# Leaving out zero products in front of four transposes in a fused attention and feed-forward kernel

## The chip, the cores and the metric

The kernel runs on one core of a Trainium2 chip. The metric is the device time of one execution in microseconds (us); unless another unit is given, every time below is in us. A core has five engines that run side by side, each with its own instruction queue worked off in order: TensorE (PE, matrix products; its weight loads are shown apart as PEld), VectorE (DVE), ScalarE (ACT), GpSimd (POOL) and SyncE (SP). Products land in PSUM, eight banks of 128 partitions; VectorE and ScalarE bring them from there to SBUF. Transfers are issued by an engine's queue and carried out by 16 DMA engines. TensorE's clock is granted by a throttle; the profile shows the granted share (1.00 is full speed).

## The reference

Attention with squared relu in place of softmax (8 batches, 12 heads, 448 positions, 64 wide), followed by a gated feed-forward layer over all 3584 tokens:

```python
scores = scale * np.matmul(q, k.transpose(0, 1, 3, 2))
attn = np.maximum(scores, 0.0) ** 2 / S
x = np.matmul(attn, v)              # heads side by side: 3584 x 768
gate = np.maximum(x @ w_gate, 0.0)
val = x @ w_val
out = (gate * val) @ w_out
```

Inputs and output are float32; the kernel computes in bfloat16 with float32 sums.

## The kernel before

The kernel goes batch by batch. A batch's heads are worked on in pairs (`hp` 0 to 5), and two pairs make a `qd` (0 to 2). q and k come in with tokens on the partitions (`qn`, `kn`) and are needed with the 64 features of a head on the partitions (`kqT`). For the first two batches TensorE makes that transposition; from the third batch on VectorE regroups the rows (`regroup`, L180, into `kr` and `qr`) and a transposing DMA on SyncE's queue does the rest.

Each batch has 21 score tiles (7 of each `qd`). A tile is four products of 64 by 64 that run together in the four quarters of TensorE's array (`mm4`), into two PSUM banks. `relu2` then takes it to SBUF: ScalarE's relu (L232) and VectorE's square (L233), which together make `attn`. `value_passes` multiplies `attn` with v, seven passes for a `qd`, and the result x is copied to SBUF (L640 by VectorE, L653 by ScalarE); `exchange` (L261) copies its halves to the other partitions. `gv_unit` makes the gate and value products from x, twelve passes for each of twelve units; L320 and L321 take them out. For later batches the attention of batch b is dealt out between the gate units of batch b-1, and the output products (`out_pair`) follow every second batch.

The change lies in `first_batch`, where no earlier batch's products fill TensorE. There the order is written out by hand, and `keep_in_program_order` holds every instruction to it. Three pairs of PSUM banks (0, 2, 4) take the tiles in turn, so that tile n can start when the relu of tile n-3 has read its banks; relu buffers `r_sb` are four, so that the relu of tile n waits for the square of tile n-4. Banks 6 and 7 take the transposes of pairs 2 to 5 in turn, and later the value products. The steps, in TensorE's order:

- twelve pairs of products of a tile of zeros (`blank`) while the first rows are loaded, then pairs 0 and 1's transposes (`first_transposes`), then four more pairs of zero products
- tiles 0 to 18, and after tiles 3, 5, 7 and 9 the transposes of pairs 2, 3, 4 and 5 (16 products with an identity, `transposes`, L208), which VectorE copies to `kqT` (L209); two pairs of zero products stand in front of each
- after tiles 12 and 17 the value products of the first and second `qd`
- tiles 19 and 20, the third `qd`'s value products and the first gate passes in between

Tile 7 is the first of `qd` 1 and needs the copies of pairs 2 and 3; tile 14 those of pairs 4 and 5. `idle_matmuls(ps, n)` issues n pairs of products, each half of the array's columns, of zeros with zeros into a bank that is overwritten afterwards; nobody reads them.

The loads are all issued by GpSimd (L116), in an order written ahead of the loops: q and k of the first batch, v, gate weights, then the second batch and more weights. They take eight semaphores in turn, so that a load is issued only when the load eight before it has landed. `load_qk(2)`, the third batch's q and k, stands right behind `first_batch` in that queue, behind the last gate weights; `regroup` of the third batch (L180) waits for it in VectorE's queue, between the second batch's squares and the gate's products.

Of the kernel before, what the change touches and what calls it, by code (L numbers as in the profile page):

```python
# [16 lines left out]
def kernel(  # L17
# [50 lines left out]
    def pin(ins):  # L68
        return tc.keep_in_program_order(ins)
# [4 lines left out]
    def mm2(o, l, r, start, stop):  # L74

        for c, p in HALVES:
            mm(o[p], l[:, p], r, start, stop)
# [124 lines left out]
    def transposes(b, hp, bank):  # L202

        ps = bank.bitcast(BF16).rearrange("p (t c) -> p t c", t=2)
        for t, nat in enumerate((kn_b[b % NB], qn_b[b % NB])):
            for i in range(4):
                for h2, half in HALVES:
                    pin(nc.tensor.transpose(ps[half, t, i * 128:i * 128 + 128], nat[:, 2 * hp + h2, i, :], ident))  # L208
        pin(nc.vector.tensor_copy(T_b[b % NB][:, :, hp, :], ps[:, :, 0:S]))  # L209

    def first_transposes(numbers):

        for n, (hp, t) in zip(numbers, ((0, 0), (0, 1), (1, 0), (1, 1))):
            ps = banks[:, n, :].bitcast(BF16)
            for i in range(4):
                for h2, half in HALVES:
                    pin(nc.tensor.transpose(ps[half, i * 128:i * 128 + 128],
                                            (kn_b, qn_b)[t][0][:, 2 * hp + h2, i, :], ident))
            o = T_b[0][:, t, hp, :]
            if (hp, t) == (1, 0):  # L220
                pin(nc.scalar.activation(o, ps[:, 0:S], AF.Copy))
            else:
                pin(nc.vector.tensor_copy(o, ps[:, 0:S]))
# [6 lines left out]
    def relu2(src, dst):  # L230
        r = rpool.tile([128, 2, S], BF16, name="r_sb")
        pin(nc.scalar.activation(r, src, AF.Relu))  # L232
        pin(nc.vector.tensor_tensor(dst, r, r, ALU.mult))  # L233
# [8 lines left out]
    def tile_of(b, n, ps):  # L242

        qd, i = divmod(n, NC)
        T = T_b[b % NB]
        a = i * 128 if i < 4 else (i - 4) * 128 + 64
        mm4([ps[:, r, :S] for r in range(2)], lambda r, c: T[:, 0, pair_of(b, 2 * qd + c), a:a + 64],
            lambda r, c: T[:, 1, pair_of(b, 2 * qd + c), :], True, True)
        return ps[:, :, :S], attn_of(b, qd)[:, 2 * i:2 * i + 2, :]

    def value_passes(b, qd, ps, i0, i1):

        attn, v_sb = attn_of(b, qd), v_b[b % NB]
        for i in range(i0, i1):
            mm4([ps[:, r, :S] for r in range(2)], lambda r, c: v_sb[:, 2 * qd + c, i, :],
                lambda r, c: attn[:, 2 * i + c, :], i == 0, i == NC - 1)

    def exchange(b, qd):
        x0, x1 = (x_of[b][e][qd] for e in range(2))
        for (_, p), (_, other) in zip(HALVES, HALVES[::-1]):  # L260
            pin(nc.vector.tensor_copy(x1[p], x0[other]))  # L261
# [19 lines left out]
    def idle_matmuls(ps, n):  # L281

        for _ in range(n):
            mm2(ps[:, :S], blank[:, 0:128], blank, True, True)
# [310 lines left out]
    def first_batch(units):  # L595


        def passes(u, n):
            for _ in range(n):
                units[u].pop(0)()  # L600

        def bank(n):
            return banks[:, n, :]

        def tile(n, at=None):
            todo.append(tile_of(0, n, sc_first() if at is None else banks[:, at:at + 2, :]))

        todo = []

        def scored():  # L610
            relu2(*todo.pop(0))

        def second_by_dve():
            src, dst = todo.pop(1)
            r = rpool.tile([128, 2, S], BF16, name="r_sb")
            pin(nc.vector.tensor_scalar(r, src, 0.0, None, ALU.max))
            scored()
            pin(nc.vector.tensor_tensor(dst, r, r, ALU.mult))

        idle_matmuls(bank(6), 12)  # L620
        first_transposes((6, 7, 5, 4))
        idle_matmuls(bank(2), 4)
        tile(0)
        tile(1)
        both = banks[:, 6:8, :]
        for n in range(2, 19):
            tile(n)
            if n in (3, 5, 7, 9):
                hp = n // 2 + 1
                idle_matmuls(bank(6 + hp % 2), 2)  # L630
                transposes(0, hp, bank(6 + hp % 2))
            if n in (12, 17):
                value_passes(0, n // 14, both, 0, NC)
            if n == 2:
                second_by_dve()
            elif n > 3:
                scored()
            if n in (12, 17):
                qd = n // 14
                pin(nc.vector.tensor_copy(x_of[0][0][qd], both[:, :, :S]))  # L640
        tile(19)
        scored()
        passes(0, 4)
        scored()
        tile(20, 0)
        scored()
        value_passes(0, 2, both, 0, 4)
        scored()
        passes(1, 4)
        value_passes(0, 2, both, 4, NC)  # L650
        exchange(0, 0)
        exchange(0, 1)
        pin(nc.scalar.activation(x_of[0][0][2], both[:, :, :S], AF.Copy))  # L653
        exchange(0, 2)
        for n in range(4):
            for u in range(2):
                passes(u, 2)
# [83 lines left out]
    new_x(0)  # L741
    units = gv_units(0)
    first_batch(units)
    load_qk(2)
    load_v(2)
# [90 lines left out]
```

## Time and profile before

| | us |
|---|---|
| median of 3 runs | 408.68 (407.84 to 408.9) |
| the profiled execution | 406.69 |
| its span, first to last instruction | 404.9 |
| TensorE busy in the span | 393.0 (97%) |
| VectorE busy | 303.9 (75%) |
| ScalarE busy | 244.3 (60%) |

A row of a timeline gives start, length, engine, line, operation, tiles written and read, and a count; a bracket gives the idle time before it and what ended that. Matmuls are pipelined, so lengths of neighbours overlap, and the distance between starts tells more of the rate than a length does. The chain of waits is the chain of work that ended last, followed back from the end: at each step to what released it. A table by stretches gives each engine's busy time and count of instructions, the granted clock and what the transfers moved.

### The profile page before, as it was taken

Reading aid. Unit: us, or ns where it says so; the run is one execution under the profiler, and the core shown is the slowest. Engines: PE = TensorE matmul, PEld = TensorE weight load, DVE = VectorE, ACT = ScalarE, POOL = GpSimd, SP = SyncE. Lnnn points to the kernel's source line nnn. Section 1 sums busy time; section 2 is a strip of 40 time slices with the busy share of each in tenths; the row PEclk is TensorE's granted clock in tenths of the full one; section 3 lists DMA queues with packets and bytes.
Section 4 is the critical chain, followed back from the end, with each engine's and each line's share of the span. In section 5 each row is a group of like instructions: output and inputs, shape, how many; then the busy total and the mean of one; then the engine's idle time right before and its main releaser. Section 6 shows DMA issues by size and latency. Waiting matters only on the chain.

```text
span 404.9 us, 16604 instructions
## 1 busy us (share of the span) xinstructions
PE 393.0 (97%) x7392; PEld 276.3 (68%) x7392; DVE 303.9 (75%) x532; ACT 244.3 (60%) x358; POOL 96.0 (24%) x164
## 2 busy tenths in 40 slices
PE   7899999999999999999999999999999999999994
PEld 3567767779776666666677677687777766777773
DVE  5985895599944786787833988988889869997651
ACT  3962984797334776877324889899873243434221
POOL 8833500610213601205244030020003120000240
PEclk9999999999999999999999999999999999999999
DMA  9999999799726993978946459561002350000154
GB/s 157 176 196 196 197 194 135 122 203 162 119 83 177 118 161 70 139 112 99 191 86 173 103 88 123 103 95 14 3 3 50 83 145 3 3 2 3 42 135 101
DMA packets 90984, 44.17 MB, mean 109 GB/s; under 512 B 55424, under 2 KB 89952, under 8 KB 90912
## 3 DMA queue, kind: packets, MB, share of 16 engines
q0 software_dynamic: 51136, 28.58, 49.5%
q1 hardware_dynamic: 39104, 13.99, 17.9%
q8 instruction: 58, 0.95, 0.9%
q10 hardware_dynamic: 672, 0.54, 0.5%
q14 instruction: 14, 0.11, 0.1%
HBM read 47.19 MB, written 11.01 MB: 144 GB/s over the span
## 4 chain that ended last, share of the span: by engine, by line
PE 79%; DVE 7%; DMA 5%; ACT 3%; issue 2%; SPq 2%; POOL 0%; DVEq 0%; ACTq 0%; POOLq 0%
PE ps L72 78%; DVE attn L233 4%; DMA kn<-in_k_dram 3%; ACT r_sb L232 3%; SPq L409 2%; DMA qn<-in_q_dram 1%; PE ps L208 1%; DMA out_dram<-attn 1%; DVE x L640 1%; DVE attn L399 0%; DVE kqT L209 0%; DVE hT L321 0%; ACT g_sb L320 0%; DVE kr L180 0%; DVE qr L180 0%
## 5 line engine op out<-in xcount | busy, mean ns | idle before, releaser
L72 PE MATMUL ps<-x,gv 64*64 64x448 bf16 x3552 | 203.5, 349 | 0.5 <-ACT r_sb L232 0.3
L72 PEld LDWEIGHTS <-gv 64*64 64x64 bf16 x4032 | 139.0, 107 | 54.8 <-issue 2.8
L232 ACT ACTIVATE r_sb<-ps 128x896 bf16<-128x896 f32 x167 | 147.9, 926 | 18.6 <-PE ps L72 15.1
L233 DVE TENSOR_TENSOR attn<-r_sb 128x896 bf16<-128x896 bf16 x167 | 102.2, 623 | 31.3 <-ACT r_sb L232 24.5
L72 PE MATMUL ps<-kqT 64*64 64x448 bf16 x672 | 67.9, 351 | 3.8 <-ACT r_sb L232 2.8
L72 PEld LDWEIGHTS <-hT 128*64 128x64 bf16 x1056 | 56.2, 110 | 20.8 <-issue 1.7
L409 POOL DMA_DIRECT2D out_dram<-attn x60 | 31.6, 531 | 154.0 <-DVE attn L399 121.2
L395 ACT ACTIVATE attn<-ps 128x384 f32<-128x384 f32 x64 | 28.9, 451 | 63.9 <-PE ps L72 63.3
L72 PE MATMUL ps<-wo,hT 128*64 128x384 bf16 (+1 forms) x720 | 53.9, 306 | 0.0
L321 DVE TENSOR_TENSOR hT<-ps,g_sb 128x448 bf16<-128x448 f32 x72 | 44.5, 619 | 9.2 <-ACT g_sb L320 8.6
L320 ACT ACTIVATE g_sb<-ps 128x448 bf16<-128x448 f32 x72 | 39.2, 546 | 18.5 <-PE ps L72 18.1
L399 DVE TENSOR_TENSOR attn<-ps,attn 128x384 f32<-128x384 f32 (+1 forms) x48 | 22.7, 503 | 33.4 <-ACT attn L395 19.4
L72 PEld LDWEIGHTS <-vn 64*64 64x64 bf16 (+1 forms) x840 | 30.9, 107 | 12.8 <-issue 2.3
L72 PEld LDWEIGHTS <-kqT 64*64 64x64 bf16 x672 | 27.0, 106 | 18.4 <-issue 8.4
L72 PE MATMUL ps<-attn,vn 64*64 64x448 bf16 x672 | 36.9, 350 | 0.1
L513 ACT ACTIVATE kqT<-ps 128x896 f32<-128x896 f32 x18 | 16.5, 918 | 25.0 <-PE ps L72 25.0
L116 POOL DMA_DIRECT2D vn<-in_v_dram x36 | 23.8, 681 | 23.0 <-DMA wo<-in_moe_w_out_dram 9.6
L677 POOL COPY flag<-kqT 128x1 bf16<-128x1 bf16 x12 | 3.1, 261 | 103.0 <-DMA kqT<-kr 75.9
L72 PE MATMUL ps<-o_ring,hT 128*64 128x384 bf16 (+1 forms) x336 | 25.8, 306 | 0.1
L517 DVE TENSOR_TENSOR kqT<-ps,kqT 128x896 f32<-128x896 f32 x18 | 19.5, 1084 | 5.9 <-PE ps L72 4.2
L266 ACT ACTIVATE x<-ps 128x448 bf16<-128x448 f32 x15 | 8.2, 544 | 14.4 <-PE ps L72 14.4
L261 DVE COPY x<-x 64x896 bf16<-64x896 bf16 x36 | 14.7, 408 | 2.0
(104 smaller groups left out, 289.4 us busy)
## 6 DMA issues: line engine op xcount, KB each, us to landing
out_dram<-attn SPq DMA_DIRECT2D x48, 96.0 KB, 2.6
out_dram<-attn POOLq DMA_DIRECT2D x46, 96.0 KB, 2.4
kn<-in_k_dram POOLq DMA_DIRECT2D x7, 384.0 KB, 5.9
qn<-in_q_dram POOLq DMA_DIRECT2D x7, 384.0 KB, 7.8
vn<-in_v_dram POOLq DMA_DIRECT2D x14, 192.0 KB, 9.1
gv<-in_moe_w_gate_dram POOLq DMA_DIRECT2D x6, 384.0 KB, 11.3
gv<-in_moe_w_val_dram POOLq DMA_DIRECT2D x6, 384.0 KB, 10.9
wo<-in_moe_w_out_dram POOLq DMA_DIRECT2D x2, 1152.0 KB, 12.3
```

The lines of the kernel that those rows point to most:

```text
L72: pin(nc.tensor.matmul(o, lhsT=l, rhs=r, start=start, stop=stop, skip_group_check=True))
L116: pin(nc.gpsimd.dma_start(out=o, in_=i))
L232: pin(nc.scalar.activation(r, src, AF.Relu))
L233: pin(nc.vector.tensor_tensor(dst, r, r, ALU.mult))
L261: pin(nc.vector.tensor_copy(x1[p], x0[other]))
L320: pin(nc.scalar.activation(g_sb, o[0], AF.Relu, scale=float(out_scale)))
L321: pin(nc.vector.tensor_tensor(hT[:, mf, col:col + S], o[1], g_sb, ALU.mult))
L395: pin(nc.scalar.activation(out_of(t, r, c), bank(P, t), AF.Copy))
L399: pin(nc.vector.tensor_tensor(o, bank(Q, t), o, ALU.add))
L409: pin(engines[c].dma_start(out=rows[:, c0:c1, :], in_=src))
L513: pin(nc.scalar.activation(held(n, j), both(PQ[n][0]), AF.Copy))
L517: pin(nc.vector.tensor_tensor(k, both(PQ[n][1]), k, ALU.add))
```

## The change

```diff
@@ -627,7 +627,6 @@
             tile(n)
             if n in (3, 5, 7, 9):
                 hp = n // 2 + 1
-                idle_matmuls(bank(6 + hp % 2), 2)
                 transposes(0, hp, bank(6 + hp % 2))
             if n in (12, 17):
                 value_passes(0, n // 14, both, 0, NC)
```

Each of the four calls issued two pairs of products of zeros, 64 columns by 448, with a weight load each: 16 products and 16 weight loads in all. The zero products at the start and ahead of tile 0 stay. No other engine has an instruction more, fewer or in another place.

## The prediction

> **What bounds the kernel now.** I read the granted clock first (1.00 throughout), then the chain of waits over the whole span:
>
> ```profile
> 12.41 0.64 DVE kqT L209
> 13.09 0.88 PE ps L72 x7
> 14.46 0.62 DVE kqT L209
> 15.08 1.07 DVE attn L233 x2
> ...
> 27.13 5.98 PE ps L72 x118
> ...
> 42.18 12.79 DMA kn<-in_k_dram
> ...
> 58.31 152.84 PE ps L72 x2926
> ```
>
> The columns are start, length, and what held the chain. Up to 14.46 the chain goes to and fro between TensorE and VectorE. From there VectorE alone sets it, squares and copies end to end, until 27.13. Then TensorE sets it, then a load of k rows for the third batch that lands at 42.18 + 12.79 = 54.97, and from 58.31 TensorE again. So the removed work lies in a stage that is bound by VectorE, and behind that stage stands a transfer.
>
> Next, TensorE's and VectorE's timelines of the first batch:
>
> ```profile
> 9.59 0.38 PE L72 MATMUL ps<-kqT 64*64 64x448 bf16 x4 [0.64 <-ACT r_sb L232]
> 9.90 0.57 PE L72 MATMUL ps<-blank 128*64 128x448 bf16 x4
> 10.30 0.39 PE L208 MATMUL ps<-ident,kn 128*64 128x128 bf16 x8
> 10.53 0.39 PE L208 MATMUL ps<-ident,qn 128*64 128x128 bf16 x8
> ```
> ```profile
> 12.41 0.62 DVE L209 COPY kqT<-ps 128x896 bf16<-128x896 bf16 x1 [0.29 <-PE ps L208]
> 12.95 1.15 DVE L233 TENSOR_TENSOR attn<-r_sb 128x896 bf16<-128x896 bf16 x2
> 14.46 0.62 DVE L209 COPY kqT<-ps 128x896 bf16<-128x896 bf16 x1 [0.36 <-PE ps L208]
> ```
>
> The lengths hold a pipeline's tail, so what a group costs TensorE is the distance between starts: 10.30 - 9.90 = 0.40 for the four zero products. The brackets say that VectorE stood idle for 0.29 and 0.36 until transposes were done. The view shows no other wait for transposes in this stage.
>
> **The change, part by part.** It removes 4 groups of 4 zero products with their weight loads, 32 TensorE instructions, and adds and moves nothing; the order on every engine is otherwise as it was. On TensorE that is 4 x 0.40 = 1.6 (9.90 to 10.30, 11.35 to 11.75, 13.40 to 13.80, 14.85 to 15.25). I followed it through the stage, start by start:
> - Pair 2's transposes may start at 9.90. Their q rows are heads 4 to 7, whose second load lands at 10.11 (issued 4.95, landing 5.16 later, in the trace's records). The eight k transposes run first, 0.23, so q's start at 10.13 and lose nothing. VectorE's copy of pair 2 goes from 10.96 to 10.89 only, as the operation before it takes until then.
> - Pair 3's transposes gain two groups, 0.80: done near 11.57 in place of 12.37. The copy follows at 11.96, behind a square, in place of 12.41: 0.45.
> - Tile 7 (13.09) waits for that copy and gains 0.45, pair 4's transposes 0.45 + 0.40 = 0.85: copy at 13.60 in place of 14.46. From here VectorE would be 0.85 ahead.
> - ScalarE must keep up. Its relus start 0.80 apart when nothing holds them. Single starts show three delays: 10.23 to 11.28 and 13.69 to 14.78 (for TensorE's tiles, 0.25 and 0.29 over) and 14.78 to 15.70 (for VectorE's square that frees a buffer, 0.13 over). They vanish, which makes 0.67; after them relus go on at 0.80 as before, and no tile comes late, since a tile follows the relu that frees its bank. The last square follows the last relu within 0.1, so the stage gains the smaller: 0.67, plus the 0.06 of slack between the two, about **0.7**. The work at 27.13 starts near 26.4.
>
> So 0.9 of the 1.6 is lost at once, to VectorE's and ScalarE's own pace. The other 0.7 meets this:
>
> ```profile
> core 0: us, PE busy (x) PEld busy (x) DVE busy (x) ACT busy (x) POOL busy (x), PEclk, DMA share, GB/s
> 16.00:28.00 12.00, 10.05 (x178) 6.12 (x171) 11.85 (x23) 10.45 (x13) 5.98 (x9) 1.00 1.46 194
> 28.00:42.00 14.00, 13.96 (x318) 10.07 (x317) 7.59 (x14) 4.23 (x8) 5.51 (x8) 1.00 1.48 196
> 42.00:55.00 13.00, 12.79 (x268) 9.21 (x263) 11.06 (x20) 12.34 (x17) 5.20 (x8) 1.00 1.48 198
> ```
> ```profile
> 54.51 0.62 DVE L233 TENSOR_TENSOR attn<-r_sb 128x896 bf16<-128x896 bf16 x1 [0.19 <-ACT r_sb L232]
> 55.10 0.56 DVE L180 COPY kr<-kn 128x1536 bf16<-128x1536 bf16 x1
> 55.57 0.62 DVE L233 TENSOR_TENSOR attn<-r_sb 128x896 bf16<-128x896 bf16 x1
> ```
>
> From 28 to 55 TensorE is full (26.75 of 27), so its work moves 0.7 earlier. At 55.10 VectorE's regrouping copy (L180) waits in its queue for the k rows of 54.97, and behind it in the same queue come a square, a product, another regrouping and a copy of x (57.65), for which TensorE waits at 58.31. The rows do not land sooner: the transfers move 194 to 198 GB/s in each stretch from 16 to 55, one load behind another, and the k load waits 12 us in that line between issue and landing. Now the copy starts 0.12 after the landing, of which about 0.05 is VectorE's own queue (its operations start 0.53 to 0.54 apart, here 0.59 after the square). So of the 0.7 no more than some **0.05** passes 55; VectorE stands idle for the rest. Nothing behind 55 changes.
>
> Sum: the profiled execution has a span of 404.9 and 1.8 around it, 406.69 in all; it becomes 406.64. It lies 2.0 under the median of the three runs shown, so I carry the difference over: 408.68 - 0.05 = 408.6. The bounds of the gain are 0 and 0.7 (if the landing did move along).
>
> **The clock.** The zero products are work for the clock gate, so their absence may cost more than they do. What the trace shows of the gate:
>
> ```profile
> 398.00:401.30 3.30, 1.44 (x24) 1.12 (x20) 0.85 (x2) 0.34 (x2) 0.00 (x0) 1.00 0.58 137
> 401.30:404.70 3.40, 0.00 (x0) 0.00 (x0) 0.00 (x0) 0.00 (x0) 0.00 (x0) 1.00 0.51 132
> 404.76:404.90 0.14, 0.00 (x0) 0.00 (x0) 0.00 (x0) 0.00 (x0) 0.00 (x0) 0.50 0.00 0
> ```
>
> A stretch with 1.44 busy of 3.30 (44%) did not cost the clock; it fell to 0.50 at 404.7, over 5 us after the last product. After the change the stretch from 9.5 to 15.2 holds 8 tiles x 0.19 and 8 x 0.225 of transposes, 3.3 of 5.7 or 58%, with no pause as long as 1. On that count it stays up, and I cost the clock at 0. But without the transposes only 1.5 of 5.7 is left, 27%, under anything that the trace shows to be enough.
> [...] No stretch of this trace has transposes without other products to tell.
>
> **The rivals.**
> 1. The gain survives 55. For it: the chain names a VectorE square as what released the issue at 41.45, so an earlier square might mean an earlier load. Against it: the 12 us in line, and the full rate. Time: 408.68 - 0.7 = 408.0.
> 2. The zero products did not run in TensorE's own time, and leaving them out moves nothing. Against it: 0.40 between starts, four times. It would give 408.7, as the forecast, so it has no chance of its own.
> 3. Slower: the clock falls somewhere between 12 and 19. Place: tiles, transposes and two blocks of value products run at half speed. Price: the zero products at the start of the span, before the clock rises, start 0.37 a pair (1.16, 1.54 and so on to 5.27) in place of 0.19, and it took some 4 us of unbroken work, from 1.16 to 5.3, for the clock to rise. Four such us from 15.2 hold six tiles and the first block of value products (7 x 0.19 = 1.3), which grows to 2.6 and holds up ScalarE, which has 0.35 to spare there (tile 13 is done at 18.57, its relu starts at 18.92): about +0.9. If the clock stays low until 27, the 7.6 of products from 15.8 (11 tiles, 21 value passes and 8 gate passes, 40 x 0.19) need 15.2 in 11.3: +3.9; and 4 more us at half speed behind 27 cost another 2. Less 0.7: +0.2 to +5.2. I take +2.0, nearer the short fall: 410.7. It is not absorbed at 55, since TensorE is full before it and VectorE has but 0.05 there. It decides once it costs more than 0.7. Only the thin 27% speaks for it; the 58% and the row of 44% speak against it.
>
> **How the numbers follow.** Forecast (no change, 408.6; own range 407.9 to 409.3) 0.48; the gain survives 0.10; the clock falls 0.42: the price of being wrong on how transposes count is one-sided, and the trace leaves that count open. A measurement here tells about 0.3% (1.2 us) from no change. Faster by more: 0.03 from the first rival's upper part and 0.02 from scatter: 0.05. Slower by more: 0.34 from the clock, 0.01 from scatter: 0.35. Within: 0.60. The range goes from 407.7 (rival 1 with some scatter) to 411.0, just over the clock's 410.7, and leaves out its long tail.
>
> **What would show it.** Right: no blank rows after 9.5; the L209 copies without TensorE idle before them, near 11.96 and 13.60; TensorE's start at 27.13 near 26.4; L180 still at 55.1 with about 0.6 of VectorE idle before it, released by the k load; 58.3 unmoved. Wrong on the landing: L180 earlier than 54.8. Wrong on the clock: a granted clock below 1.00 between 9 and 30, tiles starting 0.38 apart, and TensorE at 27.13 or later.

## The result and the profile after

The changed kernel takes 406.53 (median of 18 runs, 405.58 to 408.55), the kernel before, run beside it, 408.33 (18 runs, 406.87 to 409.97). The ratio is 0.9963 with a 95% interval of 0.9948 to 0.9977: faster by 0.37%, some 1.5 us (the two medians themselves lie 1.80 apart), where no change that can be measured was forecast. The profiled execution after has 406.18 and a span of 404.4, only 0.5 less than the profiled one of before; that one lies 0.2 under all 18 timed runs of its kernel, so the two spans alone understate the gain.

The chain of waits of the changed kernel (start, length, what held the chain):

```profile
11.81 0.55 DVE kqT L209
12.36 1.07 DVE attn L233 x2
13.42 0.60 DVE kqT L209
...
26.46 5.95 PE ps L72 x118
...
41.82 12.85 DMA kn<-in_k_dram
...
54.79 0.10 DVE kr L180
...
58.01 6.74 PE ps L72 x134
64.75 0.80 issue
65.55 169.10 PE ps L72 x3204
```

VectorE holds the chain through the transposes now: between the copies (L209) the chain no longer passes through TensorE. The load of k rows is still there, it lands at 41.82 + 12.85 = 54.67 (54.97 before), and TensorE goes on at 58.01 (58.31 before). The two lines at the end are new: TensorE stops for 0.80 at 64.75 and nothing that the profile shows releases it.

The timelines of the changed kernel show TensorE's two groups of transposes of pair 2, then VectorE's copies of pairs 3 and 4 and its regrouping (the bracket is the idle time before, and what ended it):

```profile
9.59 0.41 PE L208 MATMUL ps<-ident,kn 128*64 128x128 bf16 x8
10.20 0.41 PE L208 MATMUL ps<-ident,qn 128*64 128x128 bf16 x8 [0.20 <-DMA qn<-in_q_dram]
```
```profile
11.73 0.62 DVE L209 COPY kqT<-ps 128x896 bf16<-128x896 bf16 x1
13.40 0.62 DVE L209 COPY kqT<-ps 128x896 bf16<-128x896 bf16 x1
...
54.79 0.56 DVE L180 COPY kr<-kn 128x1536 bf16<-128x1536 bf16 x1 [0.49 <-DMA kn<-in_k_dram]
```

The zero products are gone, the brackets of 0.29 and 0.36 at the copies too, and pair 2's q rows have become a short wait, 0.20. At the regrouping the lead turns into a wait: VectorE's square before it starts 0.84 earlier than in the kernel before (53.67 against 54.51), the regrouping 0.31 earlier, as much as the load itself landed earlier. The landing differs between executions: 54.21 to 56.07 over the profiles of the kernels in which this load keeps its place. At 65.3 the same VectorE instruction comes 0.68 *later* than before, because of the 0.80. So by 65 nothing of the first batch's gain is left in this pair of traces, and yet the kernel is faster. The time comes from the other end. ScalarE's and SyncE's last issues of output stores and VectorE's last sums, before:

```profile
398.07 4.34 ACTq L409 DMA_DIRECT2D out_dram<-attn  x5
398.07 4.05 SPq L409 DMA_DIRECT2D out_dram<-attn  x5
...
398.98 0.85 DVE L399 TENSOR_TENSOR attn<-ps,attn 128x384 f32<-128x384 f32 x2 [1.87 <-PE ps L72]
```

and after:

```profile
398.50 3.15 ACTq L409 DMA_DIRECT2D out_dram<-attn  x5
398.50 3.44 SPq L409 DMA_DIRECT2D out_dram<-attn  x5
399.41 0.85 DVE L399 TENSOR_TENSOR attn<-ps,attn 128x384 f32<-128x384 f32 x2 [1.87 <-PE ps L72]
```

The work that feeds the last stores ends 0.43 later after than before, but ScalarE's five issues take 3.15 in place of 4.34. From VectorE's last sum (its second half starts 0.5 behind the row's start) to the end of the span it is 4.51 after and 5.44 before: 0.93 less. All five issues, all of one form, show which are long. ScalarE's and SyncE's issues of that stretch, before (count, then least, median and longest duration in ns, first and last start):

```profile
L409 ACTq DMA_DIRECT2D out_dram<-attn x5: 548/656/1533, 398.1 to 401.9; - x5
L409 SPq DMA_DIRECT2D out_dram<-attn x5: 549/558/1509, 398.1 to 401.6; - x5
```

and ScalarE's after:

```profile
L409 ACTq DMA_DIRECT2D out_dram<-attn x5: 552/559/608, 398.5 to 401.1; - x5
```

Before, one issue on each queue takes 1.5 where the others take 0.55 to 0.8; in the records both start at 398.7. What else runs then is told by the DMA queues of the kernel before from 398 to 400, and by the page's list of queues over the whole span (packets, MB, share of 16 engines), before and after:

```profile
q8 instruction: 1, 0.02, 3.9%
```
```profile
q8 instruction: 58, 0.95, 0.9%
```
```profile
q8 instruction: 57, 0.93, 0.9%
```

The queue that carries instructions moves one packet there, at 398.53 by the records, 1.26 long. A packet of this queue is 0.95 MB / 58 = 16 KB, and TensorE's 14784 rows in the profile (7392 products and as many weight loads; the expectations count two rows more) over 58 packets are 255 rows each; from the queue's first packet in the span to its last, by the records, TensorE starts 254.2 rows for each packet. The change takes 32 rows out of TensorE's program alone (14752 stay), and there is one packet fewer (254.3 rows for each). So I read the queue as TensorE's own program, which comes in block by block. The last one is then fetched at 390.97. A store issue on SyncE's queue takes 1.78 there too, but nothing behind it comes later for it: VectorE's sums are 0.42 behind those of before at 389 and 0.43 at 399. That a late fetch among the last stores holds up the end is the theory that the experiments came to, called D in the expectations. Theory A is the first batch's gain reaching the end after all.

### The profile page after: what moved, and what is told of

Same layout as the page of the kernel before. It is cut to its first block, busy times and chain, and to the rows that moved or that the text cites. A ratio compares the mean times of both kernels' runs of the same rounds, so it can differ in the third digit from the quotient of the medians.

```text
span 404.4 us, 16572 instructions
## 1 busy us (share of the span) xinstructions
PE 391.1 (97%) x7376; PEld 274.9 (68%) x7376; DVE 304.5 (75%) x532; ACT 244.0 (60%) x358; POOL 95.8 (24%) x164
## 4 chain that ended last, share of the span: by engine, by line
PE 86%; DVE 5%; DMA 4%; ACT 2%; issue 1%; POOL 0%; DVEq 0%; ACTq 0%
PE ps L72 85%; DMA kn<-in_k_dram 3%; DVE attn L233 2%; ACT r_sb L232 2%; DMA kr<-in_k_dram 1%; PE ps L208 1%; DVE kqT L209 1%; DVE attn L399 0%; ACT g_sb L320 0%; PE ps L217 0%; DVE kn L277 0%; DVE r_sb L616 0%; DVE x L639 0%; DVE hT L321 0%; POOL kn L116 0%
## 5 line engine op out<-in xcount | busy, mean ns | idle before, releaser
L72 PE MATMUL ps<-x,gv 64*64 64x448 bf16 x3552 | 203.3, 349 | 0.4 <-ACT r_sb L232 0.3
L72 PEld LDWEIGHTS <-gv 64*64 64x64 bf16 x4032 | 138.8, 107 | 54.5 <-issue 2.5
L72 PE MATMUL ps<-kqT 64*64 64x448 bf16 x672 | 68.3, 352 | 4.6 <-ACT r_sb L232 3.3
L72 PEld LDWEIGHTS <-hT 128*64 128x64 bf16 x1056 | 56.1, 110 | 20.9 <-issue 1.7
L72 PE MATMUL ps<-wo,hT 128*64 128x384 bf16 (+1 forms) x720 | 53.9, 306 | 0.0
L72 PEld LDWEIGHTS <-kqT 64*64 64x64 bf16 x672 | 27.5, 106 | 19.8 <-issue 9.6
L72 PEld LDWEIGHTS <-vn 64*64 64x64 bf16 (+1 forms) x840 | 30.9, 107 | 14.0 <-issue 3.4
L72 PE MATMUL ps<-attn,vn 64*64 64x448 bf16 x672 | 37.2, 350 | 0.9 <-issue 0.8
L72 PE MATMUL ps<-o_ring,hT 128*64 128x384 bf16 (+1 forms) x336 | 25.8, 306 | 0.1
```

Of the source, the lines that this page charges most:

```text
L72: pin(nc.tensor.matmul(o, lhsT=l, rhs=r, start=start, stop=stop, skip_group_check=True))
```

## The experiments

The kernels e1 to e12 were timed beside the kernel before. "Rows" are TensorE's products and weight loads in the profile; "first batch" is how much earlier than before VectorE's square near 24.6 starts; "block" is when the last block of TensorE's program is fetched; "issues" is the time of ScalarE's five last store issues; "end" runs from VectorE's last sum to the end of the span, all in the profiled execution.

| kernel | rows | first batch | block | issues | end | ratio to before |
|---|---|---|---|---|---|---|
| before | 14784 | 0 | 398.53 | 4.34 | 5.44 | |
| e1, before again | 14784 | 0.10 | 399.93 | 4.36 | 5.50 | 0.9995 [0.9978, 1.0011] |
| e5, rows added at the end | 14784 | 0.58 | 399.41 | 3.99 | 5.88 | 0.9995 [0.9978, 1.0011] |
| e7, zero products moved | 14784 | 0.36 | 399.77 | 4.14 | 5.46 | 0.9997 [0.9978, 1.0016] |
| e3, pairs 3 and 4 alone | 14768 | 0.69 | 406.98 | 3.15 | 4.56 | 0.9992 [0.9978, 1.0006] |
| e4, pairs 2 and 5 alone | 14768 | 0.78 | 406.33 | 3.15 | 4.52 | 1.0000 [0.9981, 1.0019] |
| e9, half the rows at the end | 14768 | 0.86 | 402.30 | 3.15 | 6.46 | 0.9995 [0.9979, 1.0011] |
| e10, four pairs before tile 0 | 14768 | 0.54 | 405.16 | 3.15 | 4.56 | 0.9994 [0.9978, 1.0010] |
| after | 14752 | 0.67 | 390.97 | 3.15 | 4.51 | 0.9963 [0.9948, 0.9977] |
| e2, after again | 14752 | 0.92 | 390.61 | 3.15 | 4.56 | 0.9961 [0.9946, 0.9975] |
| e6, another 32 rows | 14752 | 0.46 | 390.87 | 3.15 | 4.54 | 0.9976 [0.9956, 0.9996] |
| e8, k rows loaded earlier | 14752 | 0.81 | 394.84 | 3.15 | 4.53 | 0.9974 [0.9952, 0.9996] |
| e11, 96 rows more at the start | 14880 | 0.12 | 396.13 | 3.16 | 4.62 | 0.9981 [0.9965, 0.9996] |
| e12, the same on after | 14880 | 0.76 | 395.18 | 3.15 | 4.54 | 0.9971 [0.9958, 0.9984] |

**e1 and e2: both kernels again**, with no edit, for the spread of one profile.

> The kernel before, unchanged, against itself: the scatter of the comparison and a second trace. Ratio 1.000 within about 0.2%. Theory A (the gain made at the transposes reaches the end because in most executions nothing holds the third batch's load at 55): this trace, if its time is near the median of 408.3, shows its k rows' regrouping (L180) later than 55.1 for a reason other than the load's landing, with the load landed at least 0.5 us before. Theory B (the load's landing holds all at 55 in every execution, and the gain comes from somewhere behind it): L180 within 0.15 us of the landing again, and the 1.6 us that the median lies above the profiled execution are lost behind 60.

> The changed kernel, unchanged, a second time: ratio near 0.996. Theory A: VectorE's work at the end of the first batch some 0.7 us earlier than in the run of the kernel before, and the same 0.7 us or more still there behind 60. Theory B: nothing of it left at 58; a difference that first appears later, at places where TensorE waits for its own instructions (issue) or for a transfer.

Measured: 407.91 and 406.45 beside 407.61. The gain is there again with the same ratio, and a second profile of each gives the same end (5.50 and 4.56) but other times in between: before again is 1.48 later at 65 than the first profile of before, after again 0.34 later. The regrouping starts 0.12 behind the load's landing in both (55.53 behind 55.41, 55.12 behind 55.00), as theory B in the expectations had it. TensorE's stop near 64.75 is there in before again and not in after again. So the stop comes and goes with the execution and is not the change's; the end is the kernel's own.

**e3 and e4: one half of the change each.** e3 leaves out the zero products in front of pairs 3 and 4 (below), e4 those in front of pairs 2 and 5, with (5, 7) in the same line.

```diff
-                idle_matmuls(bank(6 + hp % 2), 2)
+                if n in (3, 9):
+                    idle_matmuls(bank(6 + hp % 2), 2)
```

> The zero products are left out in front of pairs 3 and 4 alone, those for whose transposes VectorE stood idle 0.29 and 0.36 us; 16 TensorE instructions fewer. Theory A: nearly the whole gain, ratio 0.996 to 0.998, first batch 0.6 to 0.7 us shorter. Theory C (the gain comes from TensorE's program being 32 instructions shorter, which shifts the blocks in which it is fetched): some other ratio, the same for this run and the next, each with 16 instructions fewer.

> The zero products are left out in front of pairs 2 and 5 alone, for whose transposes VectorE did not wait over 0.1 us; 16 TensorE instructions fewer as well. Theory A: at most 0.2 us shorter in the first batch (the 0.40 us of pair 2 lets the later steps start earlier, by up to that), ratio 0.999 to 1.000. Theory C: the same ratio as the run without the products of pairs 3 and 4.

Measured: both shorten the first batch by as much as the whole change does (0.69 and 0.78 against 0.67; for e4 at most 0.2 was expected), and neither is faster: 407.35 and 407.44 beside 407.61. Theory A asks for the gain in proportion to the first batch, and falls. The gain isn't a sum over the parts either: two halves of nothing make 0.37%. That looked like a step in the length of the program, and led to theory D.

**e5 and e6: the first batch and the length apart.** e5 is the changed kernel with eight pairs of zero products behind the last output products, which brings the rows back to 14784; e6 is the kernel before with another 32 rows left out.

```diff
     out_pair(B - 2, S1, apart=(S2, S3))
+    idle_matmuls(banks[:, 6, :], 8)
```
```diff
         first_transposes((6, 7, 5, 4))
-        idle_matmuls(bank(2), 4)
         tile(0)
...
-                idle_matmuls(bank(6 + hp % 2), 2)
+                if n in (5, 7):
+                    idle_matmuls(bank(6 + hp % 2), 2)
```

> The changed kernel with 8 pairs of zero products behind the last real product, where TensorE has nothing left to do: the program is as long again as before (32 TensorE instructions), the first batch as in the changed kernel. In the traces so far the kernel before fetches a last block of TensorE instructions (queue q8, 16 KB) at 398.5 and 399.9 us while the last stores are issued; two of those issues take 1.5 us in place of 0.6 to 0.8, and from VectorE's last sum to the end of the span it is 5.4 to 5.5 us; in all kernels with fewer instructions it is 4.5 to 4.6. Theory D (the block's fetch in the stores is the main part of the gain): the fetch is back near 399, the end takes 5.4 again, ratio about 0.998 to 0.999. Theory A (the first batch's gain): ratio unchanged, 0.996.

> The kernel before with 32 other TensorE instructions left out: the four pairs of zeros ahead of tile 0 and those in front of pairs 2 and 5; those in front of pairs 3 and 4 stay. Its program has the length of the changed kernel and every block behind the first batch begins at the same instruction. Theory D: ratio like the changed kernel's, 0.995 to 0.997, end 4.5 us. Theory A: at most a third of the gain, 0.998 or more.

Measured: e5 407.52, e6 406.49, beside 407.76. With the changed kernel's first batch and the old length the gain is gone; with the new length and less of a first batch (0.46) it is there. e5's added products run on TensorE behind the output products, while the stores go out, so its end alone could be their doing; that is what e7 is for.

**e7: the old length with nothing added at the end.** The four pairs of zero products stand in front of tiles 11, 12, 16 and 17 in place of the transposes.

```diff
         for n in range(2, 19):
+            if n in (11, 12, 16, 17):
+                idle_matmuls(bank(6), 2)
             tile(n)
...
-                idle_matmuls(bank(6 + hp % 2), 2)
                 transposes(0, hp, bank(6 + hp % 2))
```

> The four groups of zero products are moved, not left out: from in front of the transposes to in front of tiles 11, 12, 16 and 17, where TensorE waits 0.34 to 0.43 us for ScalarE anyway. The first batch should be as short as in the changed kernel (0.6 to 0.8 us gained at 27), the program as long as before. Theory A: ratio 0.996. Theory D: 0.999 to 1.000, end 5.4 us with the fetch in it.

Measured: 407.60 beside 407.76, ratio 0.9997, with a first batch 0.36 shorter where 0.6 to 0.8 was expected. SyncE's and ScalarE's last issues in e7:

```profile
L409 SPq DMA_DIRECT2D out_dram<-attn x7: 466/547/1697, 397.6 to 402.5; - x7
L409 ACTq DMA_DIRECT2D out_dram<-attn x5: 492/613/1037, 398.8 to 402.4; - x5
```

The slow issues, 1.70 and 1.04, are back, beside a block fetched at 399.77, and the end is 5.46, as in the kernel before. All four profiles of programs of 14784 rows have such issues among the last stores, and no other profile has.

**e8: the load moved.** The changed kernel with the third batch's k rows issued ahead of the last gate weights.

```diff
     load_gv(4)
-    load_gv(5)
...
-    load_qk(2)
+    load_nat(kn_b[0], k, 2, 0, H)
+    load_gv(5)
+    load_nat(qn_b[0], q, 2, 0, H)
```

> The changed kernel, with the last gate weights' load (2 transfers, some 4 us) moved behind the third batch's k rows, which then land near 51 in place of 54.7 to 55.0. If the load's landing is what swallows the first batch's 0.7 us, VectorE's regrouping starts 0.5 to 0.8 us earlier and the rest of the kernel with it: ratio 0.994 to 0.995 against the kernel before. If not, it stays at 0.996. The gate weights land near 55, before their first use at 58.8.

Measured: median 406.82 (404.80 to 409.56) beside 407.76. The k rows land at 51.7 in place of 55, and the regrouping no longer waits for them, it stands right behind a square:

```profile
54.25 0.63 DVE L233 TENSOR_TENSOR attn<-r_sb 128x896 bf16<-128x896 bf16 x1 [0.18 <-ACT r_sb L232]
54.79 0.55 DVE L180 COPY kr<-kn 128x1536 bf16<-128x1536 bf16 x1
```

The lead of 0.26 that the square has over the kernel before is kept (0.31 at the regrouping), where the changed kernel's fell from 0.84 to 0.31. So with the load out of the way nothing is lost here. But e8's lead of 0.81 had shrunk to 0.26 by 41 already, so the regrouping starts no earlier than in the changed kernel (54.79 in both), 0.31 ahead of the kernel before where 0.5 to 0.8 was expected. What an earlier load is worth at the end stays open: the lowest single time of all kernels is e8's 404.80, but its median (ratio 0.9974, where 0.994 to 0.995 was expected) is no better than the changed kernel's, and its profiled execution lost more right behind it. TensorE's timeline, then its table by stretches (busy time and count of PE, PEld, DVE, ACT, POOL, granted clock, DMA share, GB/s):

```profile
63.41 1.33 PE L72 MATMUL ps<-attn,vn 64*64 64x448 bf16 x24
67.22 0.39 PE L72 MATMUL ps<-attn,vn 64*64 64x448 bf16 x4 [2.48 <-issue]
```
```profile
64.06:67.47 3.41, 0.93 (x24) 0.52 (x20) 0.00 (x0) 0.00 (x0) 0.00 (x0) 1.00 1.28 118
67.47:70.89 3.42, 3.42 (x44) 2.27 (x40) 2.02 (x4) 1.09 (x2) 0.19 (x1) 0.50 1.08 150
```

TensorE stopped for 2.48 with no releaser, at the place where the changed kernel stopped for 0.80, and then ran 3.41 at half its clock; VectorE's instructions are 4.0 late from there on.

**e9 and e10: 16 rows.** e9 is e5 with four pairs at the end in place of eight; e10 leaves out only the four pairs ahead of tile 0.

```diff
     out_pair(B - 2, S1, apart=(S2, S3))
+    idle_matmuls(banks[:, 6, :], 4)
```
```diff
         first_transposes((6, 7, 5, 4))
-        idle_matmuls(bank(2), 4)
         tile(0)
```

> The changed kernel with 4 pairs of zero products behind the last real product: 16 TensorE instructions fewer than before. In the two runs with 16 fewer the last block's fetch came behind the end of the work (406 to 407 us) and the end took 4.5 us. Theory D: no fetch in the last stores, end 4.5 us, ratio as for the changed kernel, 0.995 to 0.998, although the same kind of products stands at the same place as in the run with 8 pairs (0.9995). If the products behind the end cost by themselves, it lies between, near 0.998.

> The kernel before without the four pairs of zeros ahead of tile 0, 16 TensorE instructions fewer, all others in place. Theory D: end 4.5 us, no fetch in the last stores; that alone would make 0.9975 to 0.998. The two other kernels with 16 fewer had that end and yet 0.999 and 1.000, and both lost 0.7 to 1.4 us at 131 us, where VectorE's square waits for a store and TensorE for VectorE. If that loss belongs to the place of the blocks in a program with 16 fewer, it is there again and the ratio 0.999 to 1.000; if it was chance, the ratio is 0.9975 to 0.998.

Measured: 407.87 and 407.73 beside 407.76. Theory D's forecast of a gain (0.995 to 0.998 for e9; 0.9975 to 0.998 for e10, unless a loss near 130 came with the length) is missed in both. At 14768 rows the program still has 58 blocks, the stores are issued undisturbed (ScalarE's issues take 3.15), and yet nothing is gained. The last block is fetched behind the issues: in e9 at 402.30, when the last stores are still under way. ScalarE's issue at 400.41 lands 3.98 later, where the same one of the changed kernel takes 2.12, and the span ends 6.46 after the last sum, the longest of all. In the other profiles of this length the block comes at 405 to 407, past the span's 404.4 to 405.9, and the span ends as early as the changed kernel's. e9's twelve timed runs fall in two groups, five from 406.55 to 406.91 and seven from 407.68 to 408.94. A run's time is 1.7 to 1.9 longer than its span in all runs of the other kernels whose spans are on record; in seven of the 48 runs of these four kernels it is 2.02 to 2.69 longer. So a block that is fetched in the closing may hold up the end in many executions; that rests on e9's profile and on these seven runs, and isn't shown for e3, e4 and e10. The loss near 130 that e10's expectation speaks of is no answer: between 108 and 140, e3 falls back by 1.4, e4 by 0.7 and e7 by 0.5 against the first profile of before, e9 and e10 not at all.

**e11 and e12: a longer program.** If it is the place of the last fetch that counts, and not fewer instructions, a longer program must gain as well. The twelve pairs of zero products at the very start, 448 columns wide, are cut into more and narrower ones, in the kernel before (e11, 36 pairs of 149 columns) and in the changed kernel (e12, 44 pairs of 122), both to 14880 rows.

```diff
-    def idle_matmuls(ps, n):
+    def idle_matmuls(ps, n, w=S):
-            mm2(ps[:, :S], blank[:, 0:128], blank, True, True)
+            mm2(ps[:, :w], blank[:, 0:128], blank[:, :w], True, True)
...
-        idle_matmuls(bank(6), 12)
+        idle_matmuls(bank(6), 36, 149)
```

> The kernel before, all its zero products kept, but the twelve pairs at the very start (448 columns) are cut into 36 pairs of 149 columns: about the same time on TensorE, 96 instructions more (14882 rows in place of 14786). Theory D (what counts is where the fetch of TensorE's last instruction block falls): 58 blocks as in the kernel before, but the last one is fetched some 96 instructions earlier, which at the 32 rows per us of the tail is 3 us, near 395 to 397 and ahead of the last stores; their issues take 0.6 to 0.9, the last VectorE sum starts 4.5 to 4.6 before the end of the span in place of 5.4 to 5.9, and the ratio is 0.996 to 0.998, with more instructions and no shorter first batch. A plainer theory, that fewer TensorE instructions are what gains: ratio 1.000 or above, end 5.4 or more. Theory A (the gain of the first batch reaches the end): 1.000.

> The changed kernel with the twelve pairs at the very start cut into 44 pairs of 122 columns: 14882 TensorE rows, the same program length as the other kernel of this call, but with the changed kernel's shorter first batch. Theory D: last block fetched at the same place as there, end 4.5 to 4.6, ratio 0.996 to 0.998, and the two kernels within 0.1% of each other though the first batch differs by 0.7 to 0.8. Theory A: this one shorter than the other by 0.7 to 0.8 us (0.2%).

Measured: 406.59 and 406.38 beside 407.55, ratios 0.9981 and 0.9971. e11 does all the work of the kernel before and 96 TensorE instructions more, and is faster than it. Its last block and ScalarE's last issues (DMA queues from 396 to 398, and the issues from 398 on):

```profile
q8 instruction: 1, 0.02, 4.1%
```
```profile
L409 ACTq DMA_DIRECT2D out_dram<-attn x5: 550/557/615, 398.9 to 401.5; - x5
```

The block comes at 396.13, ahead of these stores, none of the issues is long, and the end is 4.62. e12 with its shorter first batch (0.76 against 0.12) is 0.2 faster than e11, with intervals that overlap widely: if any of the first batch's gain gets through, it is no more than about that.

## Why the prediction was wrong

**The first batch: right.** Pair 3's and pair 4's copies were forecast near 11.96 and 13.60 and came at 11.73 and 13.40, with no idle time before them. The gate passes were to start near 26.4; they begin at 26.04 and go on without a break from 26.46. Some of that isn't the change's: the first q rows landed at 6.06 in this execution and 6.50 in the profiled one of before, which puts ScalarE's first relu 0.31 earlier. The q rows of pair 2 do arrive late, as seen ahead, at a cost of 0.20 on TensorE and none on VectorE, whose copy of pair 2 starts at 10.65 with no idle time before it.

**The load at 55: right in the main.** The lead of 0.84 ends in a wait of 0.49 at the regrouping, and in e8, where the load is earlier, the lead that is there (0.26) is kept. The regrouping's start of 54.79 lies just inside the prediction's own sign of being wrong on the landing (earlier than 54.8), but it follows the landing by 0.12, as it does in both repeats. The landing is at 54.8 in the mean of the ten profiles with a short first batch and at 55.5 in the three with the long one, so some of the lead may reach it; that isn't shown, as single profiles scatter by as much. Rival 1 (the gain survives 55) is answered by e3, e4, e5 and e7: a shorter first batch with no gain; between e11 and e12 up to 0.2 is possible.

**The clock: right for the forecast, and rival 3 falls.** That products of zeros are work for the clock agrees with the kernel before: from 1.16 to 5.39 TensorE has nothing but 24 of them (4.23 busy of 4.23), and the record of the full clock begins at 5.39. Without those of the change the granted clock is 1.00 from 3.9 to 403 in the changed kernel, and tiles that wait for nothing follow each other 0.19 to 0.22 apart. The rival's chance of 0.42 leaned on a comparison of two measures: its 27% counts distances between starts, and the 44% that it was held against is busy time by the profile. By that same busy time the products other than transposes fill 2.85 of the 5.70 from 9.5 to 15.2 in the changed kernel, 50%. No run shows that transposes do not count for the clock, as the 27% has it; what the runs show is the clock at 1.00 over such a stretch, in e2 with 32 transposes and 21 other products in 3.41 (1.33 and 1.68 busy).

**What failed is the sentence "Nothing behind 55 changes", and with it the sum.** The sum counted the removed instructions' time, and left out that they are also part of a program which has to be fetched. 32 rows fewer make 57 blocks out of 58; the 58th had been fetched among the last stores, where two store issues took 1.5 in place of 0.6, and the end of the span came 0.93 later behind the last sum. The page's row of 58 instruction packets, the fetch at 398.53 and the 1.53 issue were all in the trace of before. The term is shown by moving the fetch in both directions: e5 and e7 bring it back into the stores with a first batch still shorter than before (by 0.58 and 0.36), and lose the gain; e6, e11 and e12 take it out of them in three other ways, and gain. The rest of the traces bear it out. Of the 952 issues of output stores on ScalarE's and SyncE's queues in the fourteen profiles, 124 overlap a fetch of TensorE's program, and the longest take 2.0; of the 828 others none takes over 0.86. A store with a fetch under way between its issue and its landing takes 3.3 to land (median), the others 2.2. By what path a fetch slows a store isn't shown.

The base was off as well: the three runs from which the forecast of 408.6 started have a median of 408.68, all 18 of the kernel before 408.33. That is 0.35 of the 2.1 between forecast and measurement.

**What stays open.** The end accounts for 0.93. The kernels without the late fetch have medians of 406.38 to 406.59 (after, e2, e6, e11, e12; e8, with its loads in another order, 406.82), and in the comparisons of the experiments those of 14784 rows have 407.52 to 407.91: about 1.2 apart; the first comparison has it at 1.5. The 0.3 to 0.6 that are left are of the size of what one execution differs from the next: the stop near 64.75 alone (0.78 to 1.21 in six of the profiles, 2.48 in e8, none to speak of in seven), and it isn't tied to the gain, since the kernel before's profile has none. Open too is why the four kernels of 14768 rows gain nothing: their store issues are undisturbed, and only e9's profile shows its end held up.

## What to carry to other kernels

In these kernels TensorE's program came in while it ran, by the reading above, in 57 or 58 blocks of some 255 rows, and adding or removing a few instructions moved the last fetch: 96 more at the start brought it from 398.53 to 396.13, 32 fewer to 390.97 with one block less. When a change of some ten instructions moves the time more than its own path allows, compare the counts of instruction packets and look at what the last one falls on. To tell such an effect from the intended one, put the instructions back where they can't matter, or add more: here a longer program that is faster ruled out that fewer instructions are what gains. And a single pair of profiles is a poor measure at 0.4%: here they differ by 0.5 at the end, for a gain of 1.5, because the one of before was an unusually short one.

## What the runs showed of the hardware

**A stop of TensorE with no releaser.** In six profiles TensorE stops for 0.78 to 1.21 at 64.0 to 64.8, and in e8 for 2.48 at 64.74. A packet of TensorE's program is in flight shortly before each stop or as it begins (after: 62.58, 1.37 long; e8: 63.63, 1.99 long), while the transposing transfers of the third batch are under way (after: three issued from 56.84 on and three from 62.98 on, the DMA engines at 90% or more in each of the 18 slices from 58 to 63.4). In the seven profiles with a stop this packet starts at 61.83 or later; in five of the seven without it starts at 61.71 or earlier, and in e11 and e12 the packets lie elsewhere, near 58 and 65. That the stop is TensorE waiting for its own program is the likely reading; no run settles it.

**The clock falls behind a stretch that isn't idle.** In e8 it fell at 67.47, to 0.50 until 70.89, behind 3.41 us that held 24 products (0.93 busy, 27%) and no idle time longer than 2.48. At the end of the span the same shows twice: e6's clock fell at 402.56 behind 3.41 with 14 products (0.64 busy), e8's at 405.39 behind 3.41 with 22 (1.24 busy, 36%). The kernel before has 1.52 busy in the 3.41 from 397.92 and kept the clock at 1.00 there. The busy time and the longest pause go together in these stretches, so which of them counts isn't told. The length of 3.41 is that of e8's fall (67.47 to 70.89), and from the clock's rise at 6.03 to this fall lie 61.44, 18.0 times as long.

**Whether transposes hold the clock up isn't settled.** In after again (e2), a stretch of the same length, the second one from its clock's rise at 5.05 on, has fewer other products than the one behind which e8's clock fell at 67.47. Its table by stretches, the transposes (L208) alone and the other products (L72) alone:

```profile
8.47:11.88 3.41, 1.33 (x32) 1.01 (x32) 1.00 1.50 188
```
```profile
8.47:11.88 3.41, 1.68 (x21) 0.39 (x16) 1.00 1.50 188
```

21 products of 64 by 448 and 32 transposes kept the clock at 1.00, where e8's 24 such products alone lost it. By count that speaks for the transposes. By busy time it tells nothing: the 21 products alone are 1.68 busy, above the 1.52 that kept the clock with no transposes in the kernel before. No run here shows whether transposes count as the other products do.
